# An attention and mixture-of-experts kernel: POOL's work and the gathers of the first attention reordered, token weights stored by expert, the last weight sums taken in larger steps

## The chip, the cores and the metric

One core of one Trainium2 chip. The metric is the device time of one execution, in microseconds (us). Engines: PE (TensorE), DVE (VectorE), ACT (ScalarE), POOL (GpSimd), SP (SyncE, which here only issues DMAs).

## The reference

Block-sparse attention, then a dense mixture of four experts, all in float32:

```python
B, H, S, D = 4, 8, 768, 64          # 24 blocks of 32 positions
mask = |block_i - block_j| <= 1, or block 0 or 23 on either side,
       or block_j among the 3 sampled blocks of block_i
scores = where(mask, q @ k.T / sqrt(D), -1e9)
attn = softmax(scores);  x = attn @ v        # -> x: 3072 tokens x 512
p = domain_probs / domain_probs.sum(-1)
out = sum_e p[:, e] * (relu(x @ w1[e]) @ w2[e])    # 512 -> 1024 -> 512, 4 experts
```

## The kernel before

The order of the instructions on every engine is the order of the program; nothing is reordered later. Each engine works its own list in order, and waits in it hold up what is behind.

The four batches are handled one after the other. The attention of batch 0 runs alone (lines 1145 to 1224); from then on `experts()` yields small pieces of expert work, and the attention of batch b+1 is woven between pieces of batch b's.

*First attention.* There are N = 16 units: four `Edge` units (rows of the first and last block, two halves of the keys each) and twelve `Group` units (six groups t of four query blocks, the last of two, with two halves u of the heads). A unit has four stages: S (scores on PE, then reduction on DVE and exp on ACT), T (transposes on PE, copied to the tile `pt` or `ptw` by ACT and DVE), A (product with the values, scaled by DVE) and X (transposes of the result). The loop over n (line 1164) issues S of unit n, X of n-3, A of n-2 and T of n-1. `pt` has two buffers, so T of unit n writes the buffer that A of n-2 has read.

Around it the loop loads and prepares:

- `copy_k(0, t, cs)` builds the key tiles `kr` of group t by copies on POOL, with one of the three sampled blocks on ACT. There are eight key tiles, so group t+2 reuses those of group t.
- `load_q` loads a group's queries on SP; the pool has two buffers.
- `load_v0(t, c)` loads the value tile of two query blocks (window, first and last rows, and for later groups sampled rows by register) on SP, and puts the blocks whose values come by gather on the list `due`: all four of groups 0 and 1, then one of two. That is 15 gathers, and `next_gather` takes the next. A gather is an indirect DMA that POOL issues (line 213), of 128 rows of 2 KB.
- `mask_parts` makes the block indicator `ind` and clears `mask` on POOL; `place_mask` multiplies `ind` on PE at n=2 and copies to `mask`.

Line 1184: while gathers are due, POOL writes one element of the `pt` that A(n-2) has just read and then issues one gather. The write waits for A(n-2), which ties the gather to that point, and the next writer of the buffer waits for the write. Four gathers at n=1 have no such write.

*Token weights.* For batches 1 to 3 the tokens' weights are applied to the hidden layer: `first7` ends in `finish`, a relu times `pb[b, e]`, where `pb` is the weight of every token for expert e on all partitions. `token_weights` makes `pr` [128, 24, 4] (token tile, expert), `spread_weights` transposes it to `prt` in DRAM, and `load_weights(i)` reads it back, spread over the partitions, two tiles ahead.

*Sums of w2.* `sums_w2` (the generator `spare`) builds sums of w2's quarters for the seven-product scheme of batches 1 to 3: four subtractions on POOL, two splits (cast on ACT into the tile `t2` with two buffers, remainder on POOL), stores to DRAM; 14 steps for each of 2 x 8 parts. `more()` (line 1025) takes a step after every block of batch 0's expert work, and when all first-layer blocks are done (p == len(one)) a second one, whose end of the generator closes the pools of raw weights, opens the pool of `pb` and calls `load_weights(0)` and `(1)`.

Of the kernel before, what the change touches and what calls it, by code (L numbers as in the profile page):

```python
# [8 lines left out]
F32 = mybir.dt.float32  # L9
# [8 lines left out]
P = 128  # L18
# [5 lines left out]
def attention_moe_kernel(ctx: ExitStack, tc, qb, kb, vr, sampled, sampled_t, probs, w1, w2, out):  # L24


    nc = tc.nc
    B, NB = kb.shape[0], kb.shape[2]
    NT, DM = out.shape
    S = NT // B  # L30
    E = probs.shape[2]
# [4 lines left out]
    KT = S // P  # L36
    HS = S // 2
    KH = DM // P // 2
    CPE = NCH // E
# [4 lines left out]
    QG = P // BLOCK  # L44
    NG = (NB - 2 + QG - 1) // QG
# [61 lines left out]
    def blocks(t):  # L107
        return range(1 + QG * t, min(1 + QG * (t + 1), NB - 1))

    def load_q(b, t):  # L110
        js = blocks(t)
        q = gp.tile([P, QG, P], F32, name="q")
        nc.sync.dma_start(q[:, :len(js)], qb[b, :, js[0]:js[-1] + 1])
        gathered[b, t] = q, {}, {}

# [72 lines left out]
    due = []  # L188
# [7 lines left out]
    def next_gather():  # L196
        v, i, j = due.pop(0)
        gather(v, 0, i, j)
# [76 lines left out]

    def mask_parts():

        ind = p1.tile([NB, NG, P], F32, name="ind")
        nc.gpsimd.memset(ind, -BIG)
        nc.gpsimd.affine_select(out=ind, in_=ind, pattern=[[P, NG], [1, P]], compare_op=ALU.is_ge,  # L280
                                fill=0.0, base=BLOCK, channel_multiplier=-BLOCK)
        nc.gpsimd.affine_select(out=ind, in_=ind, pattern=[[-P, NG], [-1, P]], compare_op=ALU.is_ge,
                                fill=0.0, base=-1, channel_multiplier=BLOCK)
        nc.gpsimd.memset(mask, 0.0)
        mk["ind"] = ind
# [215 lines left out]
    later = {}  # L501
# [237 lines left out]
    spare = sums_w2()  # L739
# [109 lines left out]
    def load_weights(i):  # L849
        if i < (B - 1) * E:  # L850
            b, e = 1 + i // E, i % E
            pb[b, e] = later["p"].tile([P, KT, P], F32, name="pb")
            nc.sync.dma_start(pb[b, e], bass.AP(prt.tensor, prt.offset + (b * KT * E + e) * P,
                                                [[0, P], [E * P, KT], [1, P]]))

    blk = {}

    def first7(b, c, s, n):
        ps_m = later["m"]
        w, x = operand(b, c, s, n)  # L860

        def block(g, half):
            if (c, g, s) not in blk:
                blk[c, g, s] = later["a"].tile([P, 2, HS], F32, name="ha", tag="ha", bufs=7)
            return blk[c, g, s][:, half]

        def finish(half, g, src):
            q = pb[b, c // CPE].rearrange("p t k -> p (t k)")[:, g * HS:(g + 1) * HS]
            nc.vector.scalar_tensor_tensor(block(g, half), src, 0.0, q, op0=ALU.max, op1=ALU.mult)  # L869

        if c == 0:
            half, k, g = n
            i = FIRST7.index((s, half, g))
            if k == 0:
                W[0] = ps_m.tile([P, HS], F32, name="vw"[i % 2], bufs=2 - i % 2)
            product(W[0], w, x, k == 0)
            if k == 1:
                finish(half, g, W.pop(0))
            if g:
                next(weights, None)  # L880
            return
        if n in (5, 2, 3):
            v = ps_m.tile([P, HS], F32, name="v", bufs=2)
            product(v, w, x, True)
        else:
            if n == 1:
                W[s] = ps_m.tile([P, HS], F32, name="w", bufs=1)
            product(W[s], w, x, n == 1)
        if n == 2:
            nc.scalar.copy(block(0, 0), v)  # L890
        elif n == 1:
            nc.vector.tensor_add(block(0, 0), W[s], block(0, 0))
        elif n == 5:
            nc.scalar.copy(block(1, 1), v)
        elif n == 6:
            nc.vector.tensor_add(block(1, 0), W[s], block(1, 1))
            finish(0, 0, block(0, 0))
        elif n == 3:
            nc.vector.tensor_add(v, v, block(1, 0))
            finish(0, 1, v)  # L900
        elif n == 7:
            nc.vector.tensor_add(block(1, 1), W[s], block(1, 1))  # L902
        else:
            finish(1, 0, W[s])
            finish(1, 1, block(1, 1))
        next(weights, None)
# [108 lines left out]
    def experts():  # L1015
# [9 lines left out]
        def more():  # L1025

            if p > L and later.get("p") is None:
                next(spare, None)
                if p == len(one) and next(spare, None) is None:
                    only_raw.close()  # L1030
                    later["p"] = ctx.enter_context(tc.tile_pool(name="pbp", bufs=2, side="right",
                                                                reuse_waits="tile"))
                    for i in range(2):
                        load_weights(i)
# [91 lines left out]
    def spread_weights():  # L1126

        n = NT // P * E
        t = pool["a"].tile([P, P], F32, name="prt_ps", tag="a")
        nc.tensor.transpose(t[:n], pr.rearrange("p t e -> p (t e)"), ident)  # L1130
        rows = later["t"].tile([P, P], F32, name="prows", tag="t2", bufs=2)
        nc.scalar.copy(rows[:n], t[:n])
        nc.sync.dma_start(prt, rows[:n])
# [11 lines left out]
    with ExitStack() as only:  # L1145
        pool["p"] = only.enter_context(tc.tile_pool(name="pp1", bufs=3))
        pool["pt"] = only.enter_context(tc.tile_pool(name="pt1", bufs=2))
        pool["copy"] = nc.vector.tensor_copy
        pool["tag"] = "o"
        pool["t"], pool["ttag"] = pool["a"], "a"  # L1150
        pool["xg"] = 1
        pool["tcopy"] = nc.scalar.copy, nc.vector.tensor_copy
        us = units(0)
        N = len(us)
        E0 = N - 2 * NG

        rows = {0: [(0, 0), (0, 2)], 1: [(1, 0)], 2: [(1, 2)], 5: [(2, 0)], 6: [(2, 2)]}
        rows.update({2 * t + 1: [(t, 0)] for t in range(3, NG)})
        rows.update({2 * t + 2: [(t, 2)] for t in range(3, NG)})
        firsts = {2: [0], 3: [1]}  # L1160
        seconds = {3: 3, 4: 2, 6: 1, 8: 1}
        taken = 0
        row_numbers()
        for n in range(N + 3):
            if n < N:
                us[n].S()
            if n == 1:
                fill = pool["a"].tile([P, HS], F32, name="fill", tag="a")
                for _ in range(2):
                    nc.tensor.matmul(fill, zero[:, :P], zero, start=True, stop=True)  # L1170
            if 0 <= n - 3 < N:
                us[n - 3].X()
            if n == 0:
                copy_k(0, 0)
            if n == 2:
                copy_k(0, 1)
            t = (n - E0) // 2
            if n > E0 and t + 2 < NG + (n % 2 == 0):
                if n % 2:
                    load_q(0, t + 2)  # L1180
                copy_k(0, t + 2 - (n % 2 == 0), (0, 1) if n % 2 else (2, 3))
            if 0 <= n - 2 < N:
                us[n - 2].A()
                if due:

                    u = us[n - 2]
                    nc.gpsimd.memset(u.pt[:1, u.end - 1:, u.n - 1:u.n], 0.0)
                    next_gather()
            if 0 <= n - 1 < N:
                us[n - 1].T(0)  # L1190
                us[n - 1].T(1)
            if n == 2:
                place_mask()
            if n < NG - 2:
                row_blocks(n + 2)
            for t, c in rows.get(n, ()):
                load_v0(t, c)
            if n == 0:
                load_q(0, 1)
                mask_parts()  # L1200
            if n == 1:
                for _ in range(QG):
                    next_gather()
            for h in firsts.get(n, ()):
                load_w1(0, h)
            for _ in range(seconds.get(n, 0)):
                load_w2(taken)
                taken += 1
            if 0 < n < NG:
                for j in blocks(n):  # L1210
                    sampled_block(j, 1)
            if n == N - 1:
                nc.sync.dma_start(pr, probs)
            if n == N + 1:
                token_weights()
            if n == N - 4:
                pieces[0] = conversion(0)
                for _ in range(EARLY):
                    convert(0)
            if N - 7 <= n < N:  # L1220
                next(weights)
            if N - 7 <= n < N + 1 and (n - N + 7) % 2 == 0:
                split_w2((n - N + 7) // 2)
        assert taken == R2 and not due
# [113 lines left out]
```

## Time and profile before

| | |
|---|---|
| median of 3 runs | 1234.09 us (1233.68 to 1235.0) |
| profiled execution | 1232.82 us, span 1231.1 us |
| mean granted clock of PE | 0.993 |
| busy shares | PE 97%, PEld 89%, POOL 68%, DVE 66%, ACT 42% |
| first attention | 0 to 79 us; first expert product at 79.5 us |
| batch 1's experts begin | 393 us |

A row of the timeline reads: start in us, duration in us, engine, line, operation, output <- input, shapes, count, and in brackets the idle time of the engine before it with what released it. A row of the chain reads: start, duration, what. A row of waits reads: who waited <- for whom: us in total, times, longest. A window row reads: start:end, length, then busy us of PE, PEld, DVE, ACT and POOL (with counts), the granted clock of PE as a share of full speed, the DMA share and GB/s. A row on DMA gives the time from issue to landing.

### The profile page before, as it was taken

The numbers are of one execution on the slowest core, as the hardware profiler recorded it, in microseconds if no ns is written. First come the engines' busy times: TensorE is split into PE (matmuls) and PEld (weight loads), VectorE is DVE, ScalarE is ACT, GpSimd is POOL, SyncE is SP. The second block draws the span as 40 slices with busy tenths as digits, with TensorE's granted clock in tenths as the row PEclk, the third lists the DMA queues.
The fourth block names the chain that finished last, engine by engine and source line by source line (L and its number), as shares of the span: only waits on it lengthen the run. The fifth ranks groups of instructions, "written<-read, shape, count | busy, mean of one in ns | idle before, by whom it ended". The sixth has DMA issues, their size and how long they took to land.

```text
span 1231.1 us, 32030 instructions
## 1 busy us (share of the span) xinstructions
PE 1189.1 (97%) x12243; PEld 1095.4 (89%) x12243; DVE 808.7 (66%) x1701; ACT 519.8 (42%) x1259; POOL 838.4 (68%) x824
## 2 busy tenths in 40 slices
PE   7899999999999899999999999999999999999997
PEld 4678888888888898989989999989999999999997
DVE  4774757565654667767666867766566676666667
ACT  3864555656552243444533244444533333222221
POOL 7837978888776575767647775766755776666662
PEclk8999999999999899999999999999999999999999
DMA  9986869899979787888969786989876688887874
GB/s 289 264 281 232 312 246 351 290 316 318 307 266 351 227 242 233 259 278 274 270 211 345 227 267 222 286 252 283 285 253 209 219 271 266 258 262 251 255 239 154
DMA packets 214564, 326.81 MB, mean 265 GB/s; under 512 B 17483, under 2 KB 117420, under 8 KB 214412
## 3 DMA queue, kind: packets, MB, share of 16 engines
q1 hardware_dynamic: 207888, 303.53, 76.2%
q0 software_dynamic: 6480, 21.24, 5.8%
q8 instruction: 97, 1.59, 0.6%
q14 instruction: 55, 0.45, 0.1%
q10 hardware_dynamic: 44, 0.00, 0.0%
HBM read 257.02 MB, written 67.68 MB: 264 GB/s over the span
## 4 chain that ended last, share of the span: by engine, by line
PE 79%; DVE 5%; DMA 1%; issue 1%; ACT 1%; SPq 0%; POOL 0%; DVEq 0%; ACTq 0%
PE w L754 19%; PE u L991 15%; PE v L754 14%; PE v L991 12%; PE po L827 8%; PE o L396 3%; PE tp L383 2%; PE s L362 2%; PE s L355 1%; DVE ha L869 1%; PE x L415 1%; DMA pb<-prt 1%; DMA v<-in_vr_dram 1%; PE sw L433 1%; DVE tot L1001 1%
## 5 line engine op out<-in xcount | busy, mean ns | idle before, releaser
L915 POOL TENSOR_TENSOR ho<-ha,ho 128x768 fp32r<-128x768 f32 x165 | 318.3, 1938 | 244.8 <-ACT ho L914 242.0
L754 PE MATMUL w<-xo,wo 128*128 128x384 f32 x1524 | 310.9, 340 | 10.9 <-DVE ha L869 3.5
L754 PEld LDWEIGHTS w<-xo,wo 128*128 128x128 f32 x1524 | 268.8, 189 | 19.5 <-DVE ha L902 3.9
L914 ACT CAST ho<-ha 128x768 fp32r<-128x768 f32 x168 | 139.2, 837 | 269.9 <-DVE ha L869 106.1
L754 PE MATMUL v<-xo,wo 128*128 128x384 f32 x1176 | 238.9, 339 | 1.5 <-DVE xr L417 1.0
L991 PE MATMUL u<-ho,w2o 128*128 128x384 f32 x1128 | 228.2, 338 | 2.3 <-issue 2.3
L754 PEld LDWEIGHTS v<-xo,wo 128*128 128x128 f32 x1176 | 207.7, 189 | 6.4 <-DVE xr L417 1.1
L991 PEld LDWEIGHTS u<-ho,w2o 128*128 128x128 f32 x1128 | 197.0, 188 | 4.6 <-issue 2.9
L991 PE MATMUL v<-ho,w2o 128*128 128x384 f32 x888 | 179.8, 339 | 3.2 <-issue 1.5
L991 PEld LDWEIGHTS v<-ho,w2o 128*128 128x128 f32 x888 | 154.7, 188 | 7.1 <-DVE ha L869 2.7
L1001 DVE TENSOR_TENSOR tot<-v,tot 128x384 f32<-128x384 f32 x184 | 97.9, 552 | 91.6 <-PE v L991 90.3
L1001 DVE TENSOR_TENSOR tot<-u,tot 128x384 f32<-128x384 f32 x180 | 98.8, 552 | 47.9 <-PE u L991 47.8
L827 PE MATMUL po<-w2o,hh 128*128 128x512 f32 x384 | 123.5, 403 | 1.9 <-DVE oacc L842 1.9
L374 ACT ACTIVATE p<-p,mx 128x256 f32<-128x256 f32 (+1 forms) x192 | 95.3, 498 | 50.8 <-DVE mx L372 50.6
L213 POOL DMA_INDIRECT v<-in_vr_dram,vidx x81 | 79.9, 986 | 24.4 <-issue 17.8
L644 POOL TENSOR_TENSOR wo<-r,wo 128x256 fp32r<-128x256 f32 x92 | 72.4, 793 | 32.3 <-ACT wo L643 28.5
L372 DVE CUSTOM_DVE_ANT_1 p<-s,mask 128x256 f32<-128x256 f32 (+1 forms) x192 | 69.8, 419 | 22.0 <-PE s L362 17.0
L869 DVE SCALAR_TENSOR_TENSOR ha<-ha,pb 128x384 f32<-128x384 f32 x84 | 82.5, 982 | 0.0
L827 PEld LDWEIGHTS po<-w2o,hh 128*128 128x128 f32 x384 | 69.0, 188 | 12.6 <-DVE oacc L842 2.7
L827 PE MATMUL po<-w2o,hl 128*128 128x512 f32 x192 | 75.8, 395 | 0.0
L396 PEld LDWEIGHTS o<-v,pt 128*32 128x32 f32 x2816 | 46.1, 110 | 18.5 <-issue 13.5
L396 PE MATMUL o<-v,pt 128*32 128x64 f32 x2816 | 54.6, 221 | 5.1 <-issue 3.1
(169 smaller groups left out, 1627.3 us busy)
## 6 DMA issues: line engine op xcount, KB each, us to landing
w2o<-kept SPq DMA_DIRECT2D x168, 512.0 KB
wo<-kept SPq DMA_DIRECT2D x318, 256.0 KB
kept<-wo SPq DMA_DIRECT2D x106, 256.0 KB
v<-in_vr_dram SPq DMA_DIRECT2D x88, 192.0 KB
kept<-w2o SPq DMA_DIRECT2D x32, 512.0 KB
r<-in_w_dram SPq DMA_DIRECT2D x16, 512.0 KB
r<-in_w_dram SPq DMA_DIRECT2D x32, 256.0 KB
kept<-t SPq DMA_DIRECT2D x32, 256.0 KB
```

Source lines behind the costliest of these rows:

```text
L213: nc.gpsimd.indirect_dma_start(out=v[:, i, 1 - i], out_offset=None, in_=vr, element_offset=b * S * DM, in_offset=bass.IndirectOffsetOnAxis ...
L372: nc.vector.tensor_tensor_reduce(p.rearrange("p (a b) -> p a b", b=BLOCK), s[h][:n, i], mk, -SCALE, 3.0e38, ALU.add, ALU.min, mx[:n])
L374: nc.scalar.activation(p, p, AF.Exp, bias=mx[:n], scale=-1.0, accum_out=self.sums[:n, m:m + 1])
L396: nc.tensor.matmul(o[cs, m], self.pt[:, 2 * m + k, cs], vs[c][:, k, e], start=k == 0, stop=k == 1)
L644: nc.gpsimd.tensor_sub(o[:, 1], src, f32(o[:, 0]))
L754: nc.tensor.matmul(ps, w[:, wi, t], x[:, xi, t], start=fresh and m == 0, stop=m == 3 * KH - 1, skip_group_check=not fresh)
L827: nc.tensor.matmul(p, a[:, js], w[:, i], start=f == 0 and n == 0, stop=f == FT - 1 and n == 2)
L869: nc.vector.scalar_tensor_tensor(block(g, half), src, 0.0, q, op0=ALU.max, op1=ALU.mult)
L914: nc.scalar.copy(o[:, 0], src)
L915: eng.tensor_sub(o[:, 1], src, f32(o[:, 0]))
L991: nc.tensor.matmul(ps, w[:, j, wi, ds], h[:, hi, j], start=fresh and m == 0, stop=m == 5, skip_group_check=not fresh)
L1001: nc.vector.tensor_add(t, ps, t)
```

## The change

- `mask_parts` is issued ahead of the first `copy_k`, and `ind` is a tile of the rotating pool `p` in place of one of its own.
- The key copies of group 1 are issued at n=1 in place of n=2.
- Gathers: two at n=2 and two at n=3 without the one-element write, then one per iteration with it from n=4. Before: four at n=1 without it, then one per iteration with it from n=2.
- Queries: batch 0's groups 2 and 5 share a third tile `q2`; the loads move to n=2 (group 2) and n=6, 8, 10 (groups 3, 4, 5), from n=5, 7, 9, 11.
- `spread_weights` first copies `pr` to the order (expert, tile), so that a row of `pb` is 768 contiguous values in DRAM in place of six runs of 128.
- `more()` takes one more step of `spare` per call when p == len(one).

```diff
+    third = []
     def load_q(b, t):
         js = blocks(t)
-        q = gp.tile([P, QG, P], F32, name="q")
+        if b or t not in (2, 5):
+            q = gp.tile([P, QG, P], F32, name="q")
+        else:
+            if not third:
+                third.append(p1.tile([P, QG, P], F32, name="q2"))
+            q = third[0]
...
-        ind = p1.tile([NB, NG, P], F32, name="ind")
+        ind = pool["p"].tile([NB, NG, P], F32, name="ind", tag="p")
...
-            pb[b, e] = later["p"].tile([P, KT, P], F32, name="pb")
-            nc.sync.dma_start(pb[b, e], bass.AP(prt.tensor, prt.offset + (b * KT * E + e) * P,
-                                                [[0, P], [E * P, KT], [1, P]]))
+            pb[b, e] = later["p"].tile([P, S], F32, name="pb")
+            nc.sync.dma_start(pb[b, e], bass.AP(prt.tensor, prt.offset + e * NT + b * S, [[0, P], [1, S]]))
...
                 next(spare, None)
+                if p == len(one):
+                    next(spare, None)
                 if p == len(one) and next(spare, None) is None:
...
+        by_expert = later["t"].tile([P, E, NT // P], F32, name="by_expert", tag="t2", bufs=2)
+        nc.vector.tensor_copy(by_expert.rearrange("p e t -> p t e"), pr)
         t = pool["a"].tile([P, P], F32, name="prt_ps", tag="a")
-        nc.tensor.transpose(t[:n], pr.rearrange("p t e -> p (t e)"), ident)
+        nc.tensor.transpose(t[:n], by_expert.rearrange("p e t -> p (e t)"), ident)
...
             if n == 0:
+                mask_parts()
                 copy_k(0, 0)
-            if n == 2:
+            if n == 1:
                 copy_k(0, 1)
             t = (n - E0) // 2
             if n > E0 and t + 2 < NG + (n % 2 == 0):
-                if n % 2:
-                    load_q(0, t + 2)
                 copy_k(0, t + 2 - (n % 2 == 0), (0, 1) if n % 2 else (2, 3))
             if 0 <= n - 2 < N:
                 us[n - 2].A()
-                if due:
+                if due and n > 3:
                     u = us[n - 2]
                     nc.gpsimd.memset(u.pt[:1, u.end - 1:, u.n - 1:u.n], 0.0)
                     next_gather()
...
+            if n == 2 or n > 4 and n % 2 == 0 and n // 2 < NG:
+                load_q(0, 2 if n == 2 else n // 2)
...
             if n == 0:
                 load_q(0, 1)
-                mask_parts()
-            if n == 1:
-                for _ in range(QG):
-                    next_gather()
+            if n in (2, 3):
+                next_gather()
+                next_gather()
```

More of the change, by code (lines that the diff above doesn't have):

```diff
@@ L867, in finish @@
         def finish(half, g, src):
-            q = pb[b, c // CPE].rearrange("p t k -> p (t k)")[:, g * HS:(g + 1) * HS]
+            q = pb[b, c // CPE][:, g * HS:(g + 1) * HS]
             nc.vector.scalar_tensor_tensor(block(g, half), src, 0.0, q, op0=ALU.max, op1=ALU.mult)
```

## Prediction

> **What bounds the kernel now.** I read the page first, then PE's waits, then the order of time at the two places that the diff touches: the first attention (the first 79 us) and the hand-over from batch 0 to batch 1 (near 400 us).
>
> ```profile
> PE 1189.1 (97%) x12243; PEld 1095.4 (89%) x12243; DVE 808.7 (66%) x1701; ACT 519.8 (42%) x1259; POOL 838.4 (68%) x824
> PE ow L474 <- ACT ptw L463: 6.1, 2, 5.1
> PE w L754 <- DVE ha L869: 3.5, 2, 3.2
> ```
>
> PE is busy 97% of the span, so a microsecond counts only where PE stands still or is slow. The list of PE's waits has two long ones: 5.1 us in the first attention, and 3.2 us in front of batch 1's second accumulator. The change goes for both. An idle PE costs a second time, by the clock. In the windows (PE, PEld, DVE, ACT, POOL, then granted clock, DMA share, GB/s):
>
> ```profile
> 22.00:23.00 1.00, 0.00 (x0) 0.00 (x0) 0.00 (x0) 0.00 (x0) 1.00 (x5) 1.00 1.12 277
> 24.00:25.00 1.00, 0.00 (x0) 0.00 (x0) 0.00 (x0) 0.00 (x0) 1.00 (x4) 0.50 1.11 213
> 29.00:30.00 1.00, 1.00 (x6) 0.67 (x4) 0.00 (x0) 1.00 (x5) 0.79 (x1) 0.50 0.98 315
> 31.00:32.00 1.00, 1.00 (x64) 0.72 (x49) 0.46 (x3) 0.00 (x0) 0.67 (x2) 1.00 1.07 414
> ```
>
> About 2 us into the idle time the clock falls to 0.50, and it is back only after 30 us. In this stretch the matmuls are small; what that costs is read from the two values of edge units below, 0.88 us at full and 1.51 us at half clock.
>
> I number units 0 to 15 (four edges, then groups t=0..5 with two halves each), and A(i) is unit i's product with the values, made in iteration i+2. PE's order in iteration n is S(n), X(n-3), A(n-2), T(n-1).
>
> **Part 1: the early stall goes.** In order of time, before:
>
> ```profile
> 7.77 0.42 POOL L151 COPY kr<-k 128x256 f32<-128x256 f32 x1 [5.14 <-DMA k<-in_kb_dram]
> 10.84 1.29 ACT L158 COPY kr<-k 128x128 f32 x4
> 13.29 0.73 POOL L279 MEMSET ind<- 24x768 f32 x1
> 16.12 1.13 POOL L213 DMA_INDIRECT v<-in_vr_dram,vidx  x1 [0.17 <-DVE ptw L463]
> 18.41 0.88 PE L474 MATMUL ow<-vn,ptw 128*32 128x64 f32 x48
> 21.00 0.41 POOL L151 COPY kr<-k 128x256 f32<-128x256 f32 x1
> 26.44 0.09 POOL L1187 MEMSET ptw<- 1x1 f32 x1
> 26.56 0.48 ACT L463 COPY ptw<-tw 128x384 f32<-128x384 f32 x1 [5.06 <-POOL ptw L1187]
> 27.10 1.51 PE L474 MATMUL ow<-vn,ptw 128*32 128x64 f32 x48 [5.10 <-ACT ptw L463]
> ```
>
> POOL is in order: key copies (7.77 to 13.29), mask parts (13.29 to 15.95), four gathers (16.12 to 21.0), key copies of group 1 (21.0 to 26.44), and only then the memset that ties gather 4 to A(0); the copies of T(2) write that buffer, so PE waits for all of it. After: the mask parts (2.7 us) go into POOL's 5.14 us wait for the keys and cost nothing; the keys of group 1 run from 13.3 to 18.7, four gathers of 1.25 us each from 18.7 to 23.7, and neither n=2 nor n=3 has a memset. Late next are ACT and DVE: four more copies on ACT ahead of T(0)'s copy (1.29 us by the row at 10.84) push A(0), A(1) and T(2) back by about 1 us, and DVE is through with A(1)'s scaling at about 22.7, so A(2) starts at about 23.4 in place of 27.10. No idle time over 1.2 us is left, so the clock stays. From A(2) I go on with 3.3 to 3.5 us for each unit (the cycle in the next rows): A(4) at 30.0 and A(5) at 33.5.
>
> ```profile
> 35.00 1.23 PE L396 MATMUL o<-v,pt 128*32 128x64 f32 x61 [0.45 <-ACT pt L385]
> 39.25 1.10 PE L396 MATMUL o<-v,pt 128*32 128x64 f32 x64
> 41.53 0.09 POOL L1187 MEMSET pt<- 1x1 f32 x1
> 42.10 0.97 POOL L213 DMA_INDIRECT v<-in_vr_dram,vidx  x1 [0.48 <-issue]
> 43.03 1.22 PE L396 MATMUL o<-v,pt 128*32 128x64 f32 x64
> 46.23 1.10 PE L396 MATMUL o<-v,pt 128*32 128x64 f32 x64
> 71.05 0.58 PE L396 MATMUL o<-v,pt 128*32 128x64 f32 x25
> 76.59 1.09 PE L396 MATMUL o<-v,pt 128*32 128x64 f32 x32 [0.27 <-ACT pt L385]
> ```
>
> A(5) was at 39.25, so **-5.75 us** by then (-4 to -7.5: A(2) can't be before 21.7, nor need it win more than the bare idle time).
>
> **Part 2: the gathers slip by two iterations.** The words of the change say eight unbound gathers; the diff has four (two each at n=2 and n=3). The rest are still one per iteration behind a memset, from n=4 on. Before, gather k (from 0) of 4 to 14 was issued at n=k-2, now at n=k. Group t=1 needs gathers 4 to 7 in A(6), t=2 needs 9 in A(8), t=3 needs 11 in A(10), t=4 needs 13 in A(12). So each of 7, 9, 11, 13 is now issued behind the memset that waits for A(5), A(7), A(9), A(11), with the very next A as its user.
>
> From the rows: A(5) starts at 39.25, that iteration's gather at 42.10, 2.85 us later (POOL first copies keys that wait for S(7), then the memset), and A(6) followed at 43.03, 3.8 us after A(5). What is left to land in is under 1 us. Landing takes (this stretch, then all 81):
>
> ```profile
> DMA to landing us min/median/max: 4.5/5.1/7.0
> DMA to landing us min/median/max: 3.6/5.8/8.4
> ```
>
> I take 5.1, the median of the stretch. Step from A(5) to A(6): 2.85 + 5.1 = 8.0 us, likewise 7 to 8 and 9 to 10. PE has 4.0 us of work in it (A, T, S of 1.1 each, X 0.7), so it idles 4.0 us, more than the 3.2 us after which the clock fell at 400 us (rows below). That makes the next A, T and S longer by 0.63, as much again and some 0.25: 1.5 us. A(6) to A(7) is then 3.2 + 1.5 = 4.7 us. I price the clock at this and keep 0 as its other end.
>
> Gather 13 is dearer: POOL now has batch 0's first conversions in front of it.
>
> ```profile
> 63.27 1.57 ACT L525 CAST xo<-xr 128x768 fp32r<-128x768 f32 x2
> 64.19 3.61 POOL L528 TENSOR_TENSOR xo<-xr,xo 128x768 fp32r<-128x768 f32 x2 [0.80 <-ACT xo L525]
> 67.75 1.43 POOL L644 TENSOR_TENSOR wo<-r,wo 128x256 fp32r<-128x256 f32 x2
> ```
>
> Behind A(10): half-clock A and T 3.0, its copy 0.6, casts 0.8 to the first subtraction, 3.61, one 0.7, memset 0.2: gather 13 at A(10)+9.0, that is A(11)+4.3, and A(12) at A(11)+9.4. Gather 14 has a whole unit to land and costs nothing.
>
> From A(5) to A(15): 3 x 8.0 + 9.4 + 4 x 4.7 + 5.5 (71.05 to 76.59, as before) = 57.7 us, against 76.59 - 39.25 = 37.3: **+20.4 us**. Ends: at 3.6 us of landing -6.0, at 7.0 us +7.6; without the clock loss -6.0.
>
> *Weighed against a page.* The Trainium skill ("DMA: Bandwidth & Descriptors", Anatomy of one DMA) gives an end-to-end fit for such a transfer of 2.0 us plus bytes over 436 GB/s. For 256 KB that estimate is 2.6 us, below the fastest of the 81 landings here (3.6), so this trace does not agree; by it the four steps would be 10 us cheaper and the whole change about even, as in the rivals below.
>
> **Part 3: the third tile of q, loads moved on SP.** load_q(2) no longer waits for S(5) (SP stood 3.5 us there), and later groups come one iteration earlier. It removes at most the two waits of PE for q:
>
> ```profile
> PE s L352 <- DMA q<-in_qb_dram: 1.6, 2, 1.4
> ```
>
> These 1.6 us lie inside steps that the gathers now set, so I count 0 (end: -1.6, and nothing above, since what is pulled ahead, w1 and w2 behind a 256 KB load, isn't used until n=9). Putting ind into the rotation of p shifts the buffers by one, all of them read by then: 0.
>
> **Part 4: the weights of the tokens.**
>
> ```profile
> 388.56 0.62 ACT L718 CAST t<-r 128x512 fp32r<-128x512 f32 x1 [5.57 <-DMA kept<-t]
> 389.46 2.55 POOL L719 TENSOR_TENSOR r<-r,t 128x512 fp32r<-128x512 f32 x2
> 392.04 0.32 SPq L725 DMA_DIRECT2D kept<-r  x1
> 392.94 0.62 SPq L672 DMA_DIRECT2D w2o<-kept  x1
> 393.61 7.41 DMA pb<-prt
> 393.44 2.28 PE L754 MATMUL v<-xo,wo 128*128 128x384 f32 x12
> 401.12 0.56 DVE L869 SCALAR_TENSOR_TENSOR ha<-v,pb 128x384 f32<-128x384 f32 x1 [6.32 <-DMA pb<-prt]
> 403.16 4.18 PE L754 MATMUL w<-xo,wo 128*128 128x384 f32 x12 [3.20 <-DVE ha L869]
> 407.33 3.06 PE v L754 x12
> ```
>
> pb is issued at 393.61 and lands at 401.02; DVE needs 1.9 us from there to free the w bank, and PE stands from 399.96 to 403.16. Two blocks then take 4.18 and 3.06 us in place of 2.1 each on the chain: 2.85 us to the clock. Full recovery is 3.2 + 2.85 = 6.05 us, and needs pb by 398.0.
>
> Triple steps at the end (two now) bring the end of the sums to before the seventh or eighth of 17 last blocks, but the sums themselves still wait for the two t2 buffers, whose stores land at 388.5 and 389.6; so the last store stays near 392.0, and pb follows at once: 1.3 us earlier, and ahead of a 512 KB load of w2o that was in front of it. At the 400 GB/s of that time that is another 1.3 us, which gives 398.4 with no gain from the shape; 3 KB rows in place of 512 B rows have to bring only 0.4 more. I take **-6.0 us**, ends -6.05 and 0 (pb not moved). The second conversion on POOL now stands behind both L719 and ends near 393.4, at its first use: at most 0.3 us. The extra copy by_expert (one of 128x96 on DVE, once) lies beside PE: 0.
>
> **Sum**: -5.75 + 20.4 - 6.0 = **+8.6 us**, 1232.82 + 8.6 = 1241.4 for the profiled execution; the median of the runs shown is 1.27 us above it, so **1242.7 us**. Work behind 79 us is bound by PE, so both shifts reach the end.
>
> **Rivals.**
> - *Slower, by the gathers* (forecast): +8.6.
> - *The gathers land fast, the other side.* At 3.6 us each the idle times are 2.5 us, below any that dropped the clock: 3 x 6.5 + 8.5 (gather 13, with A and T at full clock) + 4 x 3.2 + 5.5 = 46.3, so +9.0 - 5.75 - 6.0 = -2.8 us: 1231.3 us. It decides below some 4.3 us of landing, and only with the clock kept at all four places. For it: DMA is less crowded while PE stands. Against: 4.5 is the least seen here.
> - *About even*: landing of 4 us with the clock falling at one of the four idle times only: -2.8 + 4 x 0.4 + 1.5 = +0.3 us, 1234.4 us.
> - *pb's wait stays*, the sums being bound by their stores: 1232.8 + 14.6 + 1.3 = 1248.7 us.
>
> **How the numbers follow.** 0.2%, 2.5 us, is about what a measurement of this kernel tells from no change. Chances: forecast 0.66, pb stays 0.13 (both slower, 0.79), even 0.11, fast landing 0.10. The range adds the landing ends (-6, +7.6) and part of the clock's to 1242.7, from the fast-landing case to 7 us landings: 1230 to 1254. The likeliest case alone is 1237 to 1250.
>
> **What would show it.** Right: A(2) at 22 to 25 us without the 5 us wait; PE idle 3 to 5 us before A(6), A(8), A(10), A(12), each time released by the DMA of v, with the clock at 0.50 behind it; first product at 90 to 97 us instead of 79.5; no wait of DVE for pb over 3 us. Wrong: those four idle times under 2 us, or gathers landing in under 4 us; then the sum turns to a gain. A DVE or ACT wait before A(2) as long as POOL's was would add what part 1 takes off.

## Result and the profile after

The changed kernel takes 1250.85 us (median of four runs, 1248.59 to 1252.06) and the kernel before 1234.22 us (four runs, 1233.68 to 1235.00): ratio 1.0127, 95% interval 1.0111 to 1.0143. It is 16.6 us slower, where 8.5 us were forecast. The profiled execution took 1252.06 us, with a span of 1250.3 us.

PE's waits after, longest in total first (total, times, longest):

```profile
PE o L403 <- DMA v<-in_vr_dram,vidx: 16.9, 6, 4.7
PE prt_ps L1140 <- DVE by_expert L1138: 3.4, 1, 3.4
PE ow L481 <- ACT ptw L470: 2.4, 2, 2.2
PE v L761 <- DMA wo<-kept: 1.0, 1, 1.0
PE w L761 <- DVE ha L875: 0.6, 1, 0.6
```

Both long waits of before are gone: 5.1 us for POOL's buffer ahead of A(2), and 3.2 us for pb (0.6 is left). (The 2.2 us that now stand under the same name are another wait, ahead of A(0) at 14.32, where before waited 1.04 us.) In their place stand 16.9 us on gathers and a wait that the prediction had at nothing, for by_expert. In order of time (start, duration, then in brackets the idle time ahead and who ended it):

```profile
22.48 0.88 PE L481 MATMUL ow<-vn,ptw 128*32 128x64 f32 x48 [0.17 <-ACT ptw L470]
34.08 1.10 PE L403 MATMUL o<-v,pt 128*32 128x64 f32 x64
42.82 1.91 PE L403 MATMUL o<-v,pt 128*32 128x64 f32 x58 [1.50 <-DMA v<-in_vr_dram,vidx]
47.84 1.10 PE L403 MATMUL o<-v,pt 128*32 128x64 f32 x64
56.60 1.77 PE L403 MATMUL o<-v,pt 128*32 128x64 f32 x52 [3.98 <-DMA v<-in_vr_dram,vidx]
69.60 1.71 PE L403 MATMUL o<-v,pt 128*32 128x64 f32 x52 [3.68 <-DMA v<-in_vr_dram,vidx]
83.75 1.71 PE L403 MATMUL o<-v,pt 128*32 128x64 f32 x52 [4.68 <-DMA v<-in_vr_dram,vidx]
88.67 1.10 PE L403 MATMUL o<-v,pt 128*32 128x64 f32 x64
94.66 1.48 PE L403 MATMUL o<-v,pt 128*32 128x64 f32 x28 [2.53 <-DMA v<-in_vr_dram,vidx]
97.28 1.58 PE L403 MATMUL o<-v,pt 128*32 128x64 f32 x32
100.72 2.36 PE L761 MATMUL v<-xo,wo 128*128 128x384 f32 x12 [1.00 <-DVE xr L424]
```

A window behind the wait of A(6) (PE, PEld, DVE, ACT, POOL, clock, DMA share, GB/s):

```profile
42.00:44.00 2.00, 1.18 (x44) 1.18 (x48) 0.59 (x3) 1.20 (x6) 0.00 (x0) 0.50 0.94 223
```

A(2) is at 22.48 and A(5) at 34.08, early as forecast. A(6), A(8), A(10) and A(12) each stand for a gather, and so does A(14). Behind the first four of these waits the matmuls take 1.7 to 1.9 us in place of 1.1: the clock has fallen to 0.50. The first expert product stands at 100.72 in place of 79.54. The gathers of this stretch landed as follows:

```profile
DMA to landing us min/median/max: 3.2/5.9/8.8
```

At the hand-over (before: pb issued at 393.61, 0.17 us behind the first product of batch 1; landed at 401.0; 3.20 us of waiting, and half clock behind it), after:

```profile
139.73 1.30 DVE L1138 COPY by_expert<-pr 128x96 f32<-128x96 f32 x1
141.09 0.31 PE L1140 MATMUL prt_ps<-ident,by_expert 128*96 128x128 f32 x1 [3.36 <-DVE by_expert L1138]
417.10 1.33 SPq L860 DMA_DIRECT2D pb<-prt  x2
417.46 0.51 PE L761 MATMUL v<-xo,wo 128*128 128x384 f32 x2
423.17 0.56 DVE L875 SCALAR_TENSOR_TENSOR ha<-v,pb 128x384 f32<-128x384 f32 x1 [4.48 <-DMA pb<-prt]
425.21 2.33 PE L761 MATMUL w<-xo,wo 128*128 128x384 f32 x12 [0.59 <-DVE ha L875]
462.09 0.56 DVE L875 SCALAR_TENSOR_TENSOR ha<-v,pb 128x384 f32<-128x384 f32 x1
```

pb goes out 0.36 us ahead of the first product and DVE has it 5.7 us behind that product, not 7.7. No half clock follows. The last row is point (c) of the ledger below.

**A ledger by stages.** I cut every profiled execution at the same four points: (a) the first expert product; (b) the first product of batch 1; (c) one of DVE's products with pb behind the hand-over, 442.83 before and 462.09 after; (d) the last of DVE's such products at full pace, 1205.87 before and 1225.13 after. Starts and differences of starts, in us, worked out from the timelines of all kernels of this study:

```
kernel        edits                                       (a)   a to b  b to c  c to d   span
before        -                                          79.54  313.90  49.39  763.04  1231.1
e2_slip_alone gathers two iterations later only         105.19  314.40  49.53  764.07  1259.8
after         all                                       100.72  316.74  44.63  763.04  1250.3
after_again   all                                        98.04  318.86  44.65  763.54  1251.7
e4_fill       all, with filler matmuls                   96.69  315.66  46.55  764.24  1249.7
e3_early_copy all, by_expert early                       96.93  315.66  44.61  767.10  1249.5
e1_eight      all, no slip (4 gathers more at n=2,3)     84.95  315.96  44.15  764.15  1234.4
e5_slip1      all, slip of one                           82.67  317.63  44.30  763.47  1233.3
e9_inter      all, no slip, by_expert early              83.18  313.32  44.52  766.79  1233.1
e10_catch     all, no slip from n=6, by_expert early     81.57  313.63  44.69  767.98  1233.1
e11_light     e10, weights loaded later                  81.41  312.66  44.81  766.54  1230.7
e6_steps      second step of the sums only               80.31  313.10  46.47  767.74  1234.2
e7_layout     weights by expert only, by_expert early    81.30  312.77  47.56  768.30  1235.2
e12_handover  both of the last two                       81.89  313.00  44.54  767.21  1233.3
```

After against before: +21.2 up to (a), +2.8 from a to b (the by_expert wait), -4.8 from b to c (the hand-over), 0.0 from c to d: +19.2, which is the difference of the two spans. (The profiled execution of before lies 1.4 us below the median of its runs and that of after 1.2 above; hence 16.6 between the medians. Each row is one execution: the two of the changed kernel differ by 2.7 us at (a) and by 2.1 from a to b, and e2's took 1261.57 us, 5.5 above the median of its runs.)

### The profile page after: what moved, and what is told of

Read it like the earlier page. It is cut to its first block, busy times and chain, and to the rows that moved or that the text cites. A ratio compares the mean times of both kernels' runs of the same rounds, so it can differ in the third digit from the quotient of the medians.

```text
span 1250.3 us, 32033 instructions
## 1 busy us (share of the span) xinstructions
PE 1195.5 (96%) x12243; PEld 1098.7 (88%) x12243; DVE 812.6 (65%) x1702; ACT 520.9 (42%) x1259; POOL 839.6 (67%) x824
## 4 chain that ended last, share of the span: by engine, by line
PE 78%; DVE 5%; DMA 3%; issue 1%; ACT 1%; POOL 0%; SPq 0%; DVEq 0%; ACTq 0%; POOLq 0%
PE w L761 19%; PE u L997 15%; PE v L761 14%; PE v L997 12%; PE po L834 8%; PE o L403 3%; PE tp L390 2%; PE s L369 2%; PE s L362 1%; DMA wo<-kept 1%; PE sw L440 1%; PE x L422 1%; PE tw L469 1%; DMA v<-in_vr_dram 1%; DVE ha L875 1%
## 5 line engine op out<-in xcount | busy, mean ns | idle before, releaser
L875 DVE SCALAR_TENSOR_TENSOR ha<-ha,pb 128x384 f32<-128x384 f32 x84 | 82.7, 984 | 0.0
L403 PEld LDWEIGHTS o<-v,pt 128*32 128x32 f32 x2816 | 50.6, 115 | 33.9 <-DMA v<-in_vr_dram,vidx 18.0
L403 PE MATMUL o<-v,pt 128*32 128x64 f32 x2816 | 60.3, 229 | 19.4 <-DMA v<-in_vr_dram,vidx 16.9
```

Of the source, the lines that this page charges most:

```text
L403: nc.tensor.matmul(o[cs, m], self.pt[:, 2 * m + k, cs], vs[c][:, k, e], start=k == 0, stop=k == 1)
```

## Experiments

My theory after the result: the slip of the gathers carries all of the loss; the early edits and the hand-over gain what was forecast. The rivals: the early edits lose something by themselves; the clock, not the landing, makes most of the price; the hand-over only moves its wait. Times of before are those of the same chip in each case, over all its runs there.

### The slip by itself: e2_slip_alone

The kernel before, with nothing changed but the places of the gathers:

```
-            if n == 1:
-                for _ in range(QG):
+            if n in (2, 3):
                 next_gather()
+                next_gather()
-                if due:
+                if due and n > 3:
```

> The kernel before with nothing but the new places of the gathers (two each at n=2 and n=3 without the write, then one per iteration from n=4). Theory: the early stall goes as well, since its write is gone, then the same five waits on gathers come; first product at 98 to 103 us, and with the old wait for pb and without the copy by_expert the time is 1252 to 1258 us. Rival (other edits carry the loss): 1228 to 1236 us.

Measured: 1256.1 us, 1.0168 of before (1.0141 to 1.0195). In order of time:

```profile
46.85 1.09 PE L396 MATMUL o<-v,pt 128*32 128x64 f32 x58 [1.83 <-DMA v<-in_vr_dram,vidx]
60.79 1.71 PE L396 MATMUL o<-v,pt 128*32 128x64 f32 x52 [2.97 <-DMA v<-in_vr_dram,vidx]
73.55 1.60 PE L396 MATMUL o<-v,pt 128*32 128x64 f32 x52 [2.96 <-DMA v<-in_vr_dram,vidx]
87.99 1.71 PE L396 MATMUL o<-v,pt 128*32 128x64 f32 x52 [5.07 <-DMA v<-in_vr_dram,vidx]
98.57 1.71 PE L396 MATMUL o<-v,pt 128*32 128x64 f32 x28 [2.93 <-DMA v<-in_vr_dram,vidx]
```

The same five users of a late gather stand, A(14) with them, and no other part of the change is there. The time is as expected; (a), at 105.19, is 2 us later than the 98 to 103 named. The slip alone makes the loss.

### The slip undone: e1_eight, e5_slip1, e9_inter

The changed kernel with four gathers at n=2 and n=3 each; with three and two; and with one behind each of group 1's key tiles, so that no two follow each other directly (this one also with by_expert copied early, below):

```
 e1:  if n in (2, 3):  for _ in range(QG): next_gather()
 e5:  if n in (2, 3):  for _ in range(5 - n): next_gather()
 e9:  if n == 1:  for c in range(QG): copy_k(0, 1, (c,)); next_gather()
      if n in (2, 3):  next_gather()
```

> The changed kernel with eight gathers without the one-element write (four each at n=2 and n=3) in place of four, so that from n=6 on every gather is issued at the same iteration as before the change. Theory (the loss is the two-iteration slip of the gathers): PE's 16.9 us of waits on the gathers vanish with the half clock behind them, the first expert product goes from 100.7 to 72-75 us and the median to 1222-1227 us. Rival (the loss comes from the other edits of the first attention: masks and keys first on POOL, four more key copies on ACT, third tile of q): the first product stays behind 95 us and the time above 1245 us.

> The changed kernel with five gathers without the write (three at n=2, two at n=3), so that gathers slip by one iteration in place of two. Theory (issue to use against a landing of 5.9 us): a gather then has a whole unit, some 5 us, more; waits of about 1 us each at A(6), A(8), A(10), A(12), too short for the clock to fall; 3 to 7 us over the kernel with eight, 1226 to 1233 us. Rival (a loss in proportion to the slip): half way between the kernel with eight and the changed one, 1236 to 1240 us.

> The changed kernel with the gathers back at their old places but without the write at n=2 and n=3, and not in one burst: at n=1 one gather of group 0 behind each of the four key tiles of group 1, one gather each at n=2 and n=3, then one per iteration with the write; also the copy by_expert moved to POOL right behind the computation of the token weights. Theory (the eight gathers in one burst slowed PE's supply, which is the 10 us that the kernel with eight lost against its sum): PE runs at its pace through S(4), T(2) and A(2), first expert product at 72 to 75 us, time 1221 to 1227 us. Rival (the slow stretch of PE at 20 to 31 us belongs to the place in PE's own program and comes whatever POOL does): first product at 79 us or later, 1230 us or more.

Measured: e1 1238.89 us, ratio 1.0036 (1.0022 to 1.0051); e5 1236.22, 1.0001 (0.9982 to 1.0021); e9 1234.8, 0.9988 (0.9971 to 1.0005). The waits on gathers are gone from all three but for one of 0.7 us in e1, and (a) falls from 98-101 to 82.7-85.0: that confirms the slip once more. But all three lie above the ranges I expected, by 3 to 12 us: the early gain isn't there, and (a) is later than before's 79.54. (e9 came out as its rival had it. e5's time lies in its rival's range, but the loss isn't in proportion to the slip: e1, without any slip, is not faster than e5.) What stands in the way shows in e1's order of time:

```profile
24.11 0.62 PE L359 MATMUL s<-kr,q 64*32 64x256 f32 x3
25.38 1.07 PE L359 MATMUL s<-kr,q 64*32 64x256 f32 x3 [0.66 <-issue]
26.84 1.04 PE L359 MATMUL s<-kr,q 64*32 64x256 f32 x3 [0.40 <-issue]
28.26 1.07 PE L359 MATMUL s<-kr,q 64*32 64x256 f32 x3 [0.38 <-issue]
```

PE makes three matmuls in 1.4 us, where all 32 of this group take 1.09 us otherwise, and nothing that the profile shows holds it ("issue"). POOL was issuing its burst of gathers just then, from 19.7 to 29.6 us in e1 and from 18.9 to 25.0 in e5, and the slow stretch ended some 1.5 to 3 us behind it; so I took the burst for its cause. e9 spreads the gathers and has the slow stretch all the same, and runs at half clock besides: the burst theory fell.

### The catch-up, and the load on the queues: e10_catch, e11_light, after_again

e10 keeps the early stretch of the changed kernel as it is and adds one gather each at n=4 and n=5. e11 is e10 with the loads of the first expert's weights moved out of that stretch. Both have by_expert copied early. after_again is the changed kernel once more.

```
 e10: if n in (4, 5):  next_gather()
 e11: firsts = {6: [0], 7: [1]};  seconds = {7: 3, 8: 2, 9: 1, 10: 1}
```

> The changed kernel with one more gather right behind the loads at n = 4 and at n = 5, so that from n = 6 on every gather goes out at the place it had before the change, while the early stretch keeps its four gathers at n = 2 and 3; the by_expert copy is made on POOL at the end of the first attention. Theory A (the slip alone costs the 21 us, and the stretch from 20 to 31 us went slowly in the earlier trials because four more gathers were added there): no gather wait of over 1 us from A(6) on, A(4) at 29 to 31, first expert product at 74 to 78 against 79.5 before, time 1224 to 1229. Rival B (TensorE is slow for some us somewhere between 20 and 30 us whenever it does not stand there, whatever the gathers do): A(4) at 33 to 38, first product at 79 to 84, time 1230 to 1236. If the gather waits stay, the slip was not it: 1245 and more.

> The kernel of e10 with the first expert's weight loads (two of w1, seven of w2, 512 KB and 256 KB each) moved from n = 2, 3, 4, 6 and 8 to n = 6 to 10, so that the DMA queues carry some 2.8 MB less between 20 and 32 us. Theory C (TensorE is slow there because the DMA engines are full, share 0.9 to 1.1 in that stretch): no pauses of TensorE without a visible releaser between 20 and 31 us, A(4) by 30, first product 1 to 6 us earlier than in e10 if e10 has the slow stretch, unless the later loads hold up the gathers. Rival D (the slow stretch does not hang on the load of the queues): the pauses are there as in e10, and the time is within 2 us of it.

> The changed kernel once more, beside the other trials on the same chip. Its first profile shows no slow stretch of TensorE between 20 and 31 us. If that stretch belongs to the program, the profile shows none again, with A(4) at 28 to 30 and 1249 to 1252 us. If it comes and goes from execution to execution, A(4) can stand at 32 to 34; behind it the waits on the gathers should then be shorter, so that the first product moves by less than 3 us and the time stays at 1249 to 1254.

Measured: e10 1234.86 us, 0.9985 (0.9968 to 1.0003); e11 1237.01, 1.0007 (0.9993 to 1.0020); after_again 1254.8, 1.0154 (1.0117 to 1.0192). In order of time, the first execution of the changed kernel, then its second:

```profile
20.57 1.09 PE L359 MATMUL s<-kr,q 64*32 64x256 f32 x32
```

```profile
21.20 2.58 PE L359 MATMUL s<-kr,q 64*32 64x256 f32 x14
24.59 1.02 PE L359 MATMUL s<-kr,q 64*32 64x256 f32 x18 [0.80 <-issue]
32.24 1.44 PE L403 MATMUL o<-v,pt 128*32 128x64 f32 x60
```

One program, two executions: the same 32 matmuls take 1.09 us in the one and 4.4 us in the other. So the slow stretch does not belong to a gather order; it comes and goes, and is in 8 of the 9 profiles that have the early edits (e1, e3, e4, e5, e9, e10, e11 and after_again; only the first of after is free of it). Nor does it need these edits: e2 has pauses of 0.5 to 1.2 us without a releaser between 24.4 and 27.1 us, and e6 and e7, with the first attention of before, have such pauses of 0.3 to 1.0 us between 19.8 and 22.4 us. In after_again the waits on gathers behind the slow stretch are shorter (15.7 us in all, 16.9 in the first) and (a) comes 2.7 us sooner, as expected; its median is 0.8 us above what I had expected.

e10 (order of time), with the gathers back and no wait on them:

```profile
21.21 0.76 PE L359 MATMUL s<-kr,q 64*32 64x256 f32 x6
22.32 0.59 PE L359 MATMUL s<-kr,q 64*32 64x256 f32 x2 [0.34 <-issue]
24.50 1.09 PE L359 MATMUL s<-kr,q 64*32 64x256 f32 x22 [0.33 <-issue]
38.33 1.14 PE L403 MATMUL o<-v,pt 128*32 128x64 f32 x64
```

A(5), the last row, is at 38.33, 0.9 us ahead of before's 39.25 and not 5. Rival B holds: of the early gain nothing reaches (a). From A(5) to (a) e10 takes 43.2 us and before 40.3; e10 has four pauses without a visible releaser there, 5.1 us together, and before has one over 0.5 us, of 1.8 us. e11 has the pauses too, between 21.6 and 24 us and again at 30 to 32. Two windows of it (PE, PEld, DVE, ACT, POOL, clock, DMA share, GB/s) show that only the second place was relieved much (e10 there: 1.05 and 386 GB/s):

```profile
22.00:24.00 2.00, 1.08 (x6) 0.50 (x5) 0.16 (x1) 1.03 (x5) 1.46 (x2) 1.00 0.83 243
30.00:32.00 2.00, 1.30 (x49) 0.90 (x46) 0.47 (x3) 0.00 (x1) 1.27 (x3) 1.00 0.80 199
```

Theory C is not borne out: PE still pauses at 0.80. With the share at 0.8 and not far lower it isn't excluded either.

### The clock's price: e4_fill

The changed kernel with two or three matmuls of zeros ahead of the products that wait:

```
+            if n in (8, 10, 12, 14, 16):
+                for _ in range(2 if n == 8 else 3): nc.tensor.matmul(fill, zero[:, :P], zero, ...)
```

> The changed kernel with two or three matmuls of zeros ahead of A in iterations 8, 10, 12, 14 and 16, which write a tile nobody reads: PE has something to do while it waits for a gather. Theory (part of the loss is the half clock after each wait: A 1.7-1.9 for 1.1, T 1.97 for 1.09, S 1.35-1.7 for 1.09): the clock stays up, 1.8 us less at each of four places and 1 us at the end, 1241 to 1245 us. Rival (only the waits count, half clock lies beside the gathers' landing): within 2 us of 1250.9. If the fills are in the way themselves: above 1252.

Measured: 1254.38 us, 1.0171 (1.0135 to 1.0208): no gain. That lies in the range named for fills that are in the way, but the changed kernel's second measurement, 1254.8 us, lies there without them. The profile can't settle the price: its gather waits sum to 7.8 us, part of them covered by the fillers; one product ran at full clock behind its wait and one did not, and the slow early stretch was there:

```profile
57.73 1.05 PE L403 MATMUL o<-v,pt 128*32 128x64 f32 x52 [2.15 <-DMA v<-in_vr_dram,vidx]
81.19 1.71 PE L403 MATMUL o<-v,pt 128*32 128x64 f32 x52 [3.56 <-DMA v<-in_vr_dram,vidx]
```

The clock's part is thus read from the first profile of after alone: in the four units behind the waits 1.7 to 2.0 us each, 7.2 us in all (below). No run tests it.

### The copy by_expert: e3_early_copy

The changed kernel, with the copy at the end of the first attention, on POOL, into a tile that is kept:

```
-    psum_e = const.tile([P, NT // P], F32, name="psum_e")
+    psum_e = p1.tile([P, NT // P], F32, name="psum_e")
+    by_expert = const.tile([P, E, NT // P], F32, name="by_expert")
...
         nc.vector.tensor_mul(pr, pr, psum_e...)
+        nc.gpsimd.tensor_copy(by_expert.rearrange("p e t -> p t e"), pr)
```

> The changed kernel with the copy by_expert made on POOL right behind the computation of the token weights, not on DVE in front of PE's transpose. Theory (PE stood 3.4 us at the transpose for that copy, at full clock behind it): 3.4 us less than the changed kernel, 1246 to 1249 us. Rival (the work behind it had slack to take the wait up): no difference, 1250 to 1252 us.

Measured: 1253.53 us, 1.0162 (1.0140 to 1.0183): not the 2 to 5 us less that I expected. The wait is gone from PE's list, and the ledger shows that this pays: from a to b the five kernels with the late copy take 317.0 us on average (315.7 to 318.9), the nine others 313.6 (312.7 to 315.7), 3.4 us less, just the wait's length. (e3 itself, at 315.66, is 1.1 and 3.2 us below the two executions of after.) The gain is given back later. From c to d the kernels with the early copy (e3, e7, e9, e10, e11, e12) take 766.5 to 768.3 us, and the seven others beside e6 763.0 to 764.2. PE's waits behind the hand-over are nearly the same in before and e12; what is longer is each block of six matmuls. In order of time, after, then e12:

```profile
1100.13 1.20 PE L997 MATMUL v<-ho,w2o 128*128 128x384 f32 x6
1113.65 1.20 PE L761 MATMUL v<-xo,wo 128*128 128x384 f32 x6
```

```profile
1099.68 1.21 PE L990 MATMUL v<-ho,w2o 128*128 128x384 f32 x6
1113.28 1.21 PE L754 MATMUL v<-xo,wo 128*128 128x384 f32 x6
```

13 blocks in 13.52 us, 1.040 each, against 13 in 13.60, 1.046 each. All six profiles with the early copy have the longer pitch and none of the others has it: from start to start, over all unbroken matmuls of this shape between 470 and 1200 us, 174.4 to 174.6 ns in the six and 173.4 to 173.5 in the eight. Between 110 and 390 us it is the other way round, 174.1 to 174.2 in the six and 175.2 to 175.4 in the eight. e12's (c) is 3.4 us ahead of before's and its (d) 0.8 us behind. That the edit costs some 4 us there is shown. Why isn't: the copy is long over. The edit also moves every later tile in the on-chip memory (384 bytes more and 96 fewer in each partition, by the shapes); whether that is the cause was not tried. (e6 lost 4.7 us from c to d without this edit: 2.6 of it in one pause of PE without a visible releaser at 842 us, and 1.6 in the second and third block behind it, which take 1.74 and 1.90 us at half clock in place of 1.04.)

### The hand-over: e6_steps, e7_layout, e12_handover

Each alone in the kernel before, and both together; e7 and e12 with the early copy.

```
 e6:   if p == len(one):  next(spare, None)        # the second step
 e7:   pb[b, e] = later["p"].tile([P, S], ...), loaded from prt.offset + e * NT + b * S, by_expert transposed
 e12:  both
```

> The kernel before with one more step of the sums per call at the end and nothing else. Theory: pb is issued some 1.3 us earlier and ahead of one load of w2o, but in runs of 512 B; it lands 1 to 2.5 us earlier, PE's wait falls from 3.2 to 1 to 2 us, and the half clock behind it may go: 1 to 4.5 us less than before. Rival (the sums are bound by their stores alone): no difference.

> The kernel before with the token weights stored by expert (rows of pb of 3 KB in place of six runs of 512 B, copy by_expert made early on POOL) and nothing else. Theory (landing 6.0 in place of 7.4 us, as between the two profiles): PE's wait falls from 3.2 to some 1.8 us, with the half clock behind it gone or not: 1.4 to 4.3 us less than before. Rival (the shape does nothing, the whole gain of the hand-over is the earlier issue): no difference.

> The kernel before with the two edits of the hand-over together (weights by expert in DRAM, with the by_expert copy made on POOL at the end of the first attention, and the second step of the sums), and nothing of the first attention's start. Theory A (the hand-over gains only when pb's load is both issued earlier and lands earlier, some 4 to 5 us as the changed kernel's own account says): 1230 to 1233 where before stands at 1234 to 1237 on the same chip, ratio 0.996 to 0.998; TensorE's wait for DVE's pb products in the second batch's first block under 1 us and no half clock after it. Rival B (each edit alone gave nothing, and the two together only move the wait to other releasers, the stored weights and the conversions on POOL): ratio 0.999 to 1.001, with over 2 us of new waits on wo or on POOL in that place.

Measured: e6 1235.92 us, 1.0008 (0.9994 to 1.0022); e7 1236.27, 1.0006 (0.9993 to 1.0019); e12 1234.41, 1.0005 (0.9987 to 1.0022). None is faster. The second accumulator's wait, e6, e7, then e12:

```profile
401.69 2.32 PE L754 MATMUL w<-xo,wo 128*128 128x384 f32 x12 [1.00 <-DVE ha L869]
```

```profile
403.05 2.92 PE L754 MATMUL w<-xo,wo 128*128 128x384 f32 x12 [2.58 <-DVE ha L868]
```

```profile
402.46 2.36 PE L754 MATMUL w<-xo,wo 128*128 128x384 f32 x12 [0.45 <-DVE ha L868]
```

From b to c the step alone takes 2.9 us off, the layout 1.8, both 4.8, the same as in the changed kernel. So the hand-over does gain, and by the sum of its two parts; e12's ratio is the one that its rival B named, but the new waits of that rival are not there: PE waits 0.45 us for DVE, and no half clock follows. In e7 and e12 the early copy takes it back from c to d; in e6 the 4.7 us above do. By the ledger e12 would be 4.2 us faster without the longer pitch, near 1230; this is worked out and wasn't run. No version that was run beats the kernel before by more than its interval; e10 comes closest.

## Why the prediction was right or wrong

The direction and the mechanism were right: slower, by gathers that are issued behind the product just ahead of their user. The size was half of the measured one, and 1250.85 us lies just above the 1237 to 1250 that was given for this case alone. By the prediction's own steps:

- *Part 1, the early stall* (-5.75 at A(5)). The first profile has A(5) at 34.08, -5.2: the chain through POOL, ACT and DVE was read rightly. That the sum came so near is partly luck: the second execution has A(5) at 37.87, -1.4. But the step "no idle time over 1.2 us is left ... from A(2) I go on with 3.3 to 3.5 us for each unit" fails in the first profile already, where PE idles for 2.2 us ahead of A(0) and the clock stayed up all the same, and in nearly every other: PE is slow for 3 to 10 us between 20 and 31 us with nothing visible to wait for. Before, PE stood from 22.00 to 27.10 anyway. With the gathers put back (e10), A(5) gains 0.9 us, and (a) nothing.
- *Part 2, the slip* (+20.4). The step from A(5) to A(6) and its three successors were put at 8.0, 8.0, 8.0 and 9.4; they took 8.7, 8.8, 8.1 and 9.0. Landing was 5.9 us in the middle and not 5.1, the clock's loss in the next step 1.7 to 2.0 where 1.5 stood (5.0, 4.9, 5.2 and 4.9 us for 4.7). These are small: +1.2 and +1.2.
- *"Gather 14 has a whole unit to land and costs nothing"* was wrong: A(14) waited 2.53 us, and from A(13) to A(15) it took 8.6 us, not 5.5. Issued at 85.77, it let A(14) go on at 94.66: the longest landing of the stage, 8.8 us, longer than a unit. +3.1.
- The rest of the stage's miss is 0.6 at A(5) and 0.5 behind A(15): in all 6.5 us, 21.2 for 14.65.
- *Part 3* (0): the two waits for q, 1.6 us, are gone from PE's list, inside steps that the gathers set.
- *Part 4, the hand-over* (-6.0): -4.8. The load went out 0.36 us ahead of the first product, PE waited 0.59 us behind it, and no half clock followed, as worked out. What was not foreseen is 1.0 us on `wo<-kept`, next in line; the 0.5 us on POOL's second conversion was put at 0.3 at most.
- *"The extra copy by_expert lies beside PE: 0"* was wrong: DVE makes it at 139.73, behind work of its own, and the transpose that PE has next in its order needs it. PE stood 3.4 us. An instruction of 1.3 us on an engine that is busy 66% of the span has a price if PE's order waits for it; I had looked at the engine's share and not at who was queued behind.

Of the signs that the prediction named, three did not come: the first product stands at 100.7 and not at 90 to 97; ahead of A(6) PE waits 1.5 us for the gather, and 2.3 us without a visible releaser just before; and DVE still waits 4.48 us for pb, where I had named 3 as the limit. That sign was badly chosen, since what counts is PE's wait behind it, 0.59 us.

The rival of gathers landing fast (1231.3 us) fell: 3.2 us was the fastest, not the rule. "pb's wait stays" (1248.7 us) came nearest to the time measured, but not by its mechanism: pb's wait went, and other terms took its place.

## What to carry to other kernels

A transfer that is issued behind a tie to an instruction costs its whole landing whenever the very next instruction of the bound engine uses it; count the units between the tie and the user, and take the slow end of the landings for those with only one. A small instruction that the bound engine's next instruction needs isn't hidden by the idle share of its own engine. And when an experiment moves a kept tile, compare a stretch that the edit can't touch: here the ledger by stages found 4 us there that the totals had hidden.

## What the hardware did that I had not expected

- *PE pauses without a visible releaser.* Three matmuls in 1.4 us for up to 10 us (e1), in one execution of a program and not in another, at 20 to 31 us. The gathers' burst does not explain it (e9), and a lighter load on the queues did not end it (e11). For the single pauses further on the traces show a pattern. In the 14 profiles there are 36 pauses of 0.5 us or more between 31.5 and 80 us; 34 of them come when PE has begun 945 to 946, 1199 to 1200, 1451 to 1453, 1699 to 1701, 1953 to 1957, 2205 to 2208 or 2711 of its matmuls and weight loads, whatever the kernel, so at places some 252 (once twice that) apart; the other two, of 0.5 us, are in e10 and e11, at 905 and 901. And the queue of instruction fetches moves 97 packets of 16.4 KB in the span, one for some 252 of PE's 24,486 matmuls and weight loads; each of the 34 pauses ends 1.2 to 1.8 us behind the end of such a packet, and e6's at 842 us 1.5 us behind one. So PE most likely waits for instructions there. That is argued from place and time; no run changes the fetches. The slow stretch at 20 to 31 us does not fit it: its pauses stand at other places, mostly between 350 and 440, and most come 2.4 to 12.5 us behind the last packet. Its cause stays open.
- *The clock at an idle time of the same length.* PE idles for 2.2 us from 12.1 us on, in after and in e9. At 16 to 17 us the clock is 1.00 in the one and 0.50 in the other (windows of after, then of e9):

```profile
16.00:17.00 1.00, 0.26 (x4) 0.28 (x3) 0.56 (x1) 1.00 (x5) 1.00 (x4) 1.00 0.99 256
```

```profile
16.00:17.00 1.00, 1.00 (x6) 1.00 (x5) 0.29 (x1) 0.19 (x1) 1.00 (x4) 0.50 0.91 205
```

The Trainium skill ("TensorE: Matmul & The Clock Gate", Part 1) says that the gate counts activity in windows that run freely and don't start with the kernel; these rows agree with that, since an equal pause had two outcomes. A single threshold for an idle time, as the prediction used it, is then a chance and not a bound.
- *The pitch of full-speed matmuls* differs by 0.6% between programs with the same instructions (1.040 and 1.046 us for six), some 4 us over a stage of 763 us. e3 differs from after in nothing but the copy and its tiles.
